# Time blocks padded to 80 rows instead of 96, first-batch inputs in arrays of their own, and routed rows kept 130 elements apart

## The chip, the cores and the metric

One NeuronCore of a Trainium2 chip runs the whole program. The metric is the device time of one execution in microseconds, taken as the median of several runs. A profile is one further execution, seen by the hardware profiler; its engines are PE (TensorE, the matrix engine), PEld (TensorE's weight loads), DVE (VectorE), ACT (ScalarE), POOL (GpSimd) and SP (SyncE, which here only issues DMAs).

## What is computed

A long convolution by FFT, a gate, and a mixture of experts with two levels of top-1 routing. Sizes: 4 batches, 10048 positions (79 blocks of 128, the last one half empty), 128 channels, 16 experts of width 1024, all in float32.

```python
h = relu(pos_emb @ w1) @ w2 * exp(-0.01 * pos)          # the filter, one for all batches
u = x * v
y = irfft(rfft(u, 2S) * rfft(h, 2S))[:S]                # along the positions
a = (x * y).reshape(B * S, D)                           # 40192 tokens
g = argmax(a @ w_group); e = argmax(a @ w_expert[g])    # with softmax weights of each
out = softmax_g * softmax_e * (relu(a @ w1[g, e]) @ w2[g, e])
```

## The kernel before

The transform is split in two steps of matmuls: one over the blocks (79 blocks, padded to `NR` rows, stand on the partitions), one over the 128 positions within a block. The program goes through these stages:

- `network` (to 43 us): the filter's small MLP for `NR` x 128 positions, in 16 groups of `4 * NR` columns. Matmuls `psh` (4 * NR columns wide) and `psg` (256 wide).
- filter transform (to 118 us): `dft_blocks` (matmuls `psa`) and `dft_positions` (`psb`), whose results DVE scales into tiles `hs`; SP stores them to `hspec` in DRAM.
- for batch b = 0 to 3, a forward stage and a middle stage. Forward: `product` loads x and v (`xv_in`) and multiplies, `fold` adds and subtracts halves into `eo`, PE does `psa`; from batch 1 on the inverse of the batch before (`inverse_blocks`, which makes `xy`, x times y) is woven in. Middle: `psb`, DVE multiplies by the filter (tiles `t`), POOL adds (`y`, lines 661 and 664), PE goes back (`pbp`, line 673) five pairs of frequencies later.
- in the middle stage of batch b + 1, `chosen` stores the rows of batch b's `xy` to DRAM (`xyd`) and computes the router; `ranked` works out each token's address. In the stages after that, `stage` loads four rows per partition of `xyd` into a tile `stg` (a unit; four buffers), POOL copies the token's number and weight beside each row (line 370) and `put` scatters the rows into pages of one expert (`prow`), by indirect DMAs of POOL.
- an inverse for the last batch (to 912 us), its routing, and from 944 us the experts, page by page.

Batch 0 differs in two ways. Its loads from channel `FIRST` (15) on go into tiles `x0` (6 channels) and `v0` (3 channels), taken out of `xv_in`, where x and v alternate in runs of 128 elements; and POOL makes two of three folds (lines 486 and 488), DVE the third.

The order of the instructions on each engine is set when the program is built: a scheduler places each instruction by what it depends on, and `keep_in_program_order`, `between` and `beyond` hold some of them to the order of the code. At run time each engine goes through its list in order. SP's list holds nearly all loads. `stage(k + 1)` is called at the first row of unit k, so a unit's copy on POOL stands ahead of the four scatters of the unit before it.

Of the kernel before, what the change touches and what calls it, by code (L numbers as in the profile page):

```python
# [12 lines left out]
F32 = mybir.dt.float32  # L13
# [11 lines left out]

SEQ, D, NB, N1 = 10048, 128, 79, 157
KM = 64
NR = 96

NN = N1 * 128  # L30
NE, G, EG, FF = 16, 4, 4, 1024
# [14 lines left out]
RW = 130  # L46
# [103 lines left out]
class Kernel:  # L150
# [60 lines left out]
    def conv(self, ctx, right):  # L211
        tc, nc, d = self.tc, self.nc, self.d
# [20 lines left out]
        xyp = ctx.enter_context(tc.tile_pool(name="xy", bufs=1, reuse_waits="tile"))  # L233
# [5 lines left out]
        for b in range(self.nbat + 1):  # L239
            last = b == self.nbat  # L240
            if last:
                ahead.close()
                inner.close()
                self.sp = ctx.enter_context(tc.tile_pool(name="stream", bufs=2, reuse_waits="tile"))
                weights = self.first_weights(right)
            if b > 0:
                xy = xyp.tile([128, NB, D], F32, tag="xy", name=f"xy{b - 1}")
            parts = groups(D, GD) if not last else []
            if b == 1:
                self.router_consts()  # L250
            self.run_ahead(b, 0, made, folded)
            for j, (d0, n) in enumerate(OUTS):
                if b > 0 and j % 2 == 0:
                    tts = self.turned(d0, min(2 * GI, D - d0))
                for i in range(2 * j, min(2 * j + 2, len(parts))):
                    self.run_ahead(b, i, made, folded)
                    self.scatter(1 + (i >= 12 and i % 2))
                    self.dft_blocks(*folded[i])
                    if b > 0 and i % 2 == 0:
                        if j % 2 == 0:  # L260
                            pos = self.inverse_rest(min(2 * GI, D - d0), tts)
                        self.inverse_blocks(b - 1, xy, d0, n, tts, pos[j % 2], j % 2)
                if last:
                    if j % 2 == 0:
                        pos = self.inverse_rest(min(2 * GI, D - d0), tts)
                    self.inverse_blocks(b - 1, xy, d0, n, tts, pos[j % 2], j % 2)
                    next(weights, None)
                    if j == 8:
                        self.scatter(sum(1 for s in self.scatters if s[0] < self.nbat - 2))
                        self.all[0].load(self.rows)  # L270
                for _ in range(3 if last else 1):
                    next(routing, None)
                if last:
                    self.scatter(1 + j % 2)
            made, folded = [], []
            if b > 0:
                oh = self.rp.tile([128, NE, NB], F32, tag="oh", name="oh")
                en = self.entries.tile([128, NB, 2], F32, tag="en", name="en")
                routing = chain(self.chosen(b - 1, xy, oh, en), self.ranked(b - 1, oh, en))
                if last:  # L280
                    for _ in range(CHOSEN):
                        next(routing)
            if not last:
                back = []
                for i, (k0, n) in enumerate(groups(NB, 2)):
                    back.append(self.middle(b, k0, n))
                    if len(back) > LAG:
                        self.back(*back.pop(0))
                    if b == 1 and i % 4 == 1:
                        self.clear_rest(i // 4)  # L290
                    self.scatter(i % 4 != 3, False)
                    if i % 4 != 3 if i < 30 else i in (31, 33):
                        next(routing, None)
                    if i >= 36:
                        self.run_ahead(b + 1, i - 36 - AHEAD - 1, made, folded)
                for args in back:
                    self.back(*args)
                for _ in range(2):
                    next(routing, None)
# [60 lines left out]
    def stage(self, k):  # L360

        while self.staged <= min(k, len(self.units) - 1):
            u = self.units[self.staged]
            n = u.n
            u.rows = self.entries.tile([128, UB, RW], F32, tag="stg", name="stg", bufs=STG)
            src = self.d["xyd"][u.b * 128 * NB : (u.b + 1) * 128 * NB].rearrange("(p t) c -> p t c", p=128)
            ins = self.nc.sync.dma_start(u.rows[:, :n, 0:128], src[:, u.t0 : u.t0 + n])
            if self.sent is not None:
                self.after(ins, self.sent)
            self.beyond(self.nc.gpsimd.tensor_copy(u.rows[:, :n, 128:130], u.en[:, u.t0 : u.t0 + n]))  # L370
            self.staged += 1
# [72 lines left out]
    def product(self, b, d0, n):  # L444

        nc, d = self.nc, self.d
        src = d["xv_in"][b, :, d0 : d0 + n]
        if b == 0 and d0 >= FIRST:

            queue = nc.gpsimd if d0 < FIRST + GI else nc.sync  # L450
            if (d0 - FIRST) % GI == 0:
                self.x0 = self.ap.tile([NR, GI, 128], F32, tag="load", name="x0", bufs=NLOAD)
                m = min(GI, D - d0)
                queue.dma_start(self.x0[:, :m], d["xv_in"][b, :, d0 : d0 + m, 0])
            tag, bufs = ("spec", NSPEC) if d0 // GD % 9 < 4 else ("tt", NTT)
            vt = self.sp.tile([NR, GD, 128], F32, tag=tag, name="v0", bufs=bufs)[:, :n]
            queue.dma_start(vt, src[:, :, 1])
            o = (d0 - FIRST) % GI
            xt = self.x0[:, o : o + n]
        else:  # L460
            xv = self.ap.tile([NR, GD, 2, 128], F32, tag="load", name="xv", bufs=NLOAD)
            nc.sync.dma_start(xv[:, :n], src)
            xt, vt = xv[:, :n, 0], xv[:, :n, 1]
            if b > 0:
                self.minus[d0] = xv[:, :n].rearrange("p d a q -> p d (a q)")
        first = b == 0 and d0 < FIRST
        self.in_turn(b, (nc.gpsimd if first else nc.vector).tensor_tensor(xt, xt, vt, ALU.mult))
        return xt, b, d0, n
# [327 lines left out]
    def chosen(self, b, xy, oh, en):  # L796


        nc, d, rp = self.nc, self.d, self.rp
# [4 lines left out]
        for u in range(len(units) + 2):  # L804
            if u < len(units):
                t0, n = units[u]
                nc.sync.dma_start(rows[:, t0 : t0 + n], xy[:, t0 : t0 + n])
                pt = self.psT.tile([128, 4, 128], F32, tag="pt", name="ptr")
                for i in range(n):
                    nc.tensor.transpose(pt[:, i], xy[:, t0 + i], self.ident)  # L810
                xts[u] = self.sp.tile([128, 4, 128], F32, tag="oo", name="xrt", bufs=2)
                nc.scalar.copy(xts[u][:, :n], pt[:, :n])
            if 0 < u <= len(units):

                n, xt = units[u - 1][1], xts.pop(u - 1)
# [12 lines left out]
            if u > 1:  # L828
                t0, n = units[u - 2]
# [27 lines left out]
    def ranked(self, b, oh, en):  # L857
# [92 lines left out]
        flat = lambda t: t.rearrange("p e t -> p (e t)")  # L950
        for h in range(4):
            es = slice(h * 4, h * 4 + 4)
            f = rp.tile([128, 4, NB], F32, tag="big1", name="f")


            first = oh[:, es, 0:1].rearrange("p e t -> p (e t)")
# [272 lines left out]
class Idle:  # L1229

    real, n, steps = False, 1, 4
# [161 lines left out]
def build(nbat):  # L1393
    import concourse.bacc as bacc

    nc = bacc.Bacc("TRN2", target_bir_lowering=False, num_devices=1, dynamic_dma_scratch_size=8192)
    shapes = {
        "xv_in": (nbat, NR, D, 2, 128),
        "x_out": (nbat, 128, D * NB),
        "pos_t": (128, 64 * NR),  # L1400
        "p_w1": (128, 128),
        "p_w2": (128, 256),
        "w_router": (128, 32),
        "m_w1": (128, NE, FF),
        "m_w2": (128, NE, FF),
        "c_iota": (128, 2 + NE + sum(PZ)),
    }
    for n, a in make_consts().items():
        shapes[n] = a.shape
    d = {n: nc.dram_tensor(n, s, F32, kind="ExternalInput").ap() for n, s in shapes.items()}  # L1410
    d["out"] = nc.dram_tensor("out", (nbat * 128 * NB, D), F32, kind="ExternalOutput").ap()
    d["prow"] = nc.dram_tensor("prow", (Pages(nbat).n * TP, RW), F32, kind="Internal").ap()
    d["xyd"] = nc.dram_tensor("xyd", (nbat * 128 * NB, D), F32, kind="Internal").ap()
    d["hspec"] = nc.dram_tensor("hspec", (128, NB, 2, 128), F32, kind="Internal").ap()
    with tile.TileContext(nc) as tc:
        Kernel(tc, d, nbat).emit()
    return nc


def layout(x, v, pos_emb, w1, w2, moe_w_group, moe_w_expert, moe_w1, moe_w2):  # L1420
# [21 lines left out]
    def twice(a):  # L1442
# [2 lines left out]

    m = {
        "xv_in": c(np.stack([xb[:, :, q], vb[:, :, q]]).transpose(1, 2, 4, 0, 3)),
        "x_out": c(
            np.concatenate(
                [xb[:, :NB, p][..., chan[d0 : d0 + n]].transpose(0, 2, 1, 3).reshape(nbat, 128, -1) for d0, n in OUTS], 2  # L1450
# [36 lines left out]
```

## Time and profile before

| | us |
|---|---|
| median of 3 runs | 1947.93 (1946.37 to 1948.35) |
| profiled execution, its own time | 1945.94 |
| span of the profiled execution | 1944.2 |
| PE busy in it | 1852.0 |
| DVE, ACT, POOL busy in it | 1458.0, 1317.4, 1086.7 |

The span runs from the first to the last instruction; the 1.7 us between it and the execution's own time lie around it. Busy times are sums over stages with different limits; matmuls overlap one another, so that a busy PE need not be a full one. The profiled execution was 2.0 us faster than the median of the runs.

### The profile page before, as it was taken

The numbers are of one execution on the slowest core, as the hardware profiler recorded it, in microseconds if no ns is written. First come the engines' busy times: TensorE is split into PE (matmuls) and PEld (weight loads), VectorE is DVE, ScalarE is ACT, GpSimd is POOL, SyncE is SP. The second block draws the span as 40 slices with busy tenths as digits, with TensorE's granted clock in tenths as the row PEclk, the third lists the DMA queues.
The fourth block names the chain that finished last, engine by engine and source line by source line (L and its number), as shares of the span: only waits on it lengthen the run. The fifth ranks groups of instructions, "written<-read, shape, count | busy, mean of one in ns | idle before, by whom it ended". The sixth has DMA issues, their size and how long they took to land.

```text
span 1944.2 us, 44476 instructions
## 1 busy us (share of the span) xinstructions
PE 1852.0 (95%) x14494; PEld 1567.9 (81%) x14494; DVE 1458.0 (75%) x3102; ACT 1317.4 (68%) x3017; POOL 1086.7 (56%) x1225
## 2 busy tenths in 40 slices
PE   8988999989999899978899999999999999999997
PEld 7966878778877687766788888888888888899997
DVE  6577767688768976893789777777777777778885
ACT  6653378447843685446777777777777777788886
POOL 3237710664799568967255556666664333355554
PEclk9999999999999999999899999999999999999999
DMA  4599976988998799857653344444343222234332
GB/s 145 199 283 252 306 188 191 350 267 263 282 326 289 233 265 343 302 186 241 218 194 112 118 128 127 164 133 131 121 131 98 90 94 97 79 119 128 122 121 77
DMA packets 234433, 365.19 MB, mean 188 GB/s; under 512 B 29687, under 2 KB 113634, under 8 KB 234192
## 3 DMA queue, kind: packets, MB, share of 16 engines
q1 hardware_dynamic: 198960, 286.90, 47.9%
q0 software_dynamic: 25728, 59.82, 8.9%
q10 hardware_dynamic: 9504, 15.54, 2.9%
q8 instruction: 117, 1.92, 0.4%
q14 instruction: 124, 1.02, 0.2%
HBM read 272.15 MB, written 91.03 MB: 187 GB/s over the span
## 4 chain that ended last, share of the span: by engine, by line
PE 66%; DVE 10%; DMA 4%; ACT 4%; issue 3%; POOL 2%; SPq 0%; ACTq 0%; DVEq 0%; POOLq 0%
PE ph L1334 8%; PE ph L1336 8%; PE py L1354 8%; PE ph L1335 8%; PE py L1356 8%; PE py L1355 8%; PE psb L497 4%; PE pbp L673 3%; PE ptm L1368 2%; PE px L1289 2%; PE po L728 2%; DMA xv<-xv_in 2%; PE po L707 2%; DMA bt<-c_b 1%; DVE t L660 1%
## 5 line engine op out<-in xcount | busy, mean ns | idle before, releaser
L1343 DVE SCALAR_TENSOR_TENSOR hl<-ph,hh 128x512 fp32r<-128x512 f32 x656 | 450.4, 687 | 172.1 <-ACT hh L1342 167.2
L1380 POOL DMA_INDIRECT out<-os,to x328 | 324.6, 990 | 384.1 <-ACT os L1375 309.6
L1342 ACT ACTIVATE hh<-ph 128x512 fp32r<-128x512 f32 x656 | 395.4, 603 | 157.5 <-PE ph L1336 134.8
L378 POOL DMA_INDIRECT prow<-stg,adr x316 | 326.3, 1032 | 122.6 <-issue 53.9
L1334 PE MATMUL ph<-xh,wh 128*128 128x512 f32 (+1 forms) x808 | 301.2, 373 | 2.2 <-ACT wh L1316 2.2
L1336 PE MATMUL ph<-xh,wl 128*128 128x512 f32 (+1 forms) x808 | 284.4, 352 | 0.0
L1354 PE MATMUL py<-hh,wh 128*128 128x512 f32 (+1 forms) x808 | 283.5, 351 | 0.0
L1335 PE MATMUL ph<-xl,wh 128*128 128x512 f32 (+1 forms) x808 | 283.4, 351 | 0.0
L1356 PE MATMUL py<-hh,wl 128*128 128x512 f32 (+1 forms) x808 | 283.0, 350 | 0.0
L1355 PE MATMUL py<-hl,wh 128*128 128x512 f32 (+1 forms) x808 | 282.2, 349 | 0.0
L661 POOL TENSOR_TENSOR y<-t 128x256 f32<-128x256 f32 (+1 forms) x160 | 121.1, 757 | 141.0 <-DVE t L660 136.4
L412 PE MATMUL psa<-fa,eo 96*64 96x158 f32 x2048 | 182.1, 305 | 12.6 <-POOL eo L486 5.7
L680 ACT COPY z<-pbp 128x512 f32<-128x512 f32 x128 | 74.8, 585 | 160.5 <-PE pbp L673 155.7
L673 PE MATMUL pbp<-y,bp 128*128 128x256 f32 x632 | 164.7, 384 | 12.7 <-POOL y L664 12.7
L497 PE MATMUL psb<-z,bt 128*128 128x256 f32 x640 | 161.8, 384 | 10.6 <-DMA bt<-c_b 3.9
L1336 PEld LDWEIGHTS ph<-xh,wl 128*128 128x128 f32 x808 | 153.6, 190 | 21.2 <-DVE wl L1323 0.2
L1355 PEld LDWEIGHTS py<-hl,wh 128*128 128x128 f32 x808 | 153.2, 190 | 20.9
L1356 PEld LDWEIGHTS py<-hh,wl 128*128 128x128 f32 x808 | 153.1, 189 | 20.7
L1354 PEld LDWEIGHTS py<-hh,wh 128*128 128x128 f32 x808 | 153.0, 189 | 20.3
L412 PEld LDWEIGHTS psa<-fa,eo 96*64 96x64 f32 x2048 | 143.2, 138 | 32.0 <-POOL eo L486 9.2
L1334 PEld LDWEIGHTS ph<-xh,wh 128*128 128x128 f32 x808 | 154.0, 191 | 17.3 <-ACT wh L1316 2.4
L1335 PEld LDWEIGHTS ph<-xl,wh 128*128 128x128 f32 x808 | 154.5, 191 | 14.9
(233 smaller groups left out, 3771.4 us busy)
## 6 DMA issues: line engine op xcount, KB each, us to landing
ws<-m_w SPq DMA_DIRECT2D x202, 256.0 KB
ht<-hspec SPq DMA_DIRECT2D x156, 256.0 KB
xv<-xv_in SPq DMA_DIRECT2D x131, 288.0 KB
bt<-c_b SPq DMA_DIRECT2D x95, 256.0 KB
bp<-c_bp SPq DMA_DIRECT2D x76, 256.0 KB
xyd<-xy SPq DMA_DIRECT2D x76, 256.0 KB
stg<-xyd SPq DMA_DIRECT2D x76, 256.0 KB
xg<-prow SPq DMA_DIRECT2D x63, 260.0 KB
```

The source lines that it names most:

```text
L378: ins = self.nc.gpsimd.indirect_dma_start(self.d["prow"], bass.IndirectOffsetOnAxis(ap=u.adr[:, t : t + 1], axis=0), u.rows[:, t - u.t0], ...
L412: ins = nc.tensor.matmul(ps[hs, i], eo[:, i, hs], self.fa[:, h], start=True, stop=True)
L497: nc.tensor.matmul(ps[:, i].rearrange("p s d -> p d s"), bt[:, i], self.frequency(k0 + i, 1)[:, :, 0], start=True, stop=True,)
L1334: k.fix(nc.tensor.matmul(ph[:, j], wh, self.xh, start=True, stop=False))
L1335: k.fix(nc.tensor.matmul(ph[:, j], wh, self.xl, start=False, stop=False))
L1336: k.fix(nc.tensor.matmul(ph[:, j], wl, self.xh, start=False, stop=True))
L1342: k.fix(nc.scalar.activation(hh, ph, AF.Relu))
L1343: k.fix(nc.vector.scalar_tensor_tensor(hl, ph, 0.0, hh.bitcast(F32), ALU.max, ALU.subtract))
L1354: k.fix(nc.tensor.matmul(self.py, wh, hh, start=(c == 0), stop=False))
L1355: k.fix(nc.tensor.matmul(self.py, wh, hl, start=False, stop=False))
L1356: k.fix(nc.tensor.matmul(self.py, wl, hh, start=False, stop=(c == NC - 1)))
L1380: ins = k.nc.gpsimd.indirect_dma_start(k.d["out"], bass.IndirectOffsetOnAxis(ap=self.to[:, h : h + 1], axis=0), o, None, bounds_check=k.nt ...
```

## The change

`NR` becomes 80. That changes the width of `psh` and of the operations around it from 384 to 320 columns, the rows of every load of x and v and of `pos_t` and `c_win`, and the rows of the transform's first step from 96 to 80. Batch 0 reads x and v from `x0_in` and `v0_in`, in which a partition's channels follow each other, so that a load moves one run of 3072 or 1536 bytes per partition instead of runs of 512. `xy`, `xyd` and the load into `stg` get rows of 130 elements; the two added columns are set to 0 by a memset on POOL, once per batch, and a load into `stg` moves one run of 2080 bytes per partition instead of four of 512. The tile `f` of `ranked` shares the memory of `lg` instead of having its own.

```diff
-NR = 96
+NR = 80
...
             if b > 0:
-                xy = xyp.tile([128, NB, D], F32, tag="xy", name=f"xy{b - 1}")
+                xy = xyp.tile([128, NB, RW], F32, tag="xy", name=f"xy{b - 1}")
+                nc.gpsimd.memset(xy[:, :, D:], 0.0)
...
             src = self.d["xyd"][u.b * 128 * NB : (u.b + 1) * 128 * NB].rearrange("(p t) c -> p t c", p=128)
-            ins = self.nc.sync.dma_start(u.rows[:, :n, 0:128], src[:, u.t0 : u.t0 + n])
+            ins = self.nc.sync.dma_start(u.rows[:, :n], src[:, u.t0 : u.t0 + n])
             if self.sent is not None:
                 self.after(ins, self.sent)
             self.beyond(self.nc.gpsimd.tensor_copy(u.rows[:, :n, 128:130], u.en[:, u.t0 : u.t0 + n]))
...
-                queue.dma_start(self.x0[:, :m], d["xv_in"][b, :, d0 : d0 + m, 0])
+                queue.dma_start(self.x0[:, :m], d["x0_in"][:, d0 : d0 + m])
...
-            queue.dma_start(vt, src[:, :, 1])
+            queue.dma_start(vt, d["v0_in"][:, d0 : d0 + n])
...
-                    nc.tensor.transpose(pt[:, i], xy[:, t0 + i], self.ident)
+                    nc.tensor.transpose(pt[:, i], xy[:, t0 + i, 0:D], self.ident)
...
-            f = rp.tile([128, 4, NB], F32, tag="big1", name="f")
+            f = rp.tile([128, 4, NB], F32, tag="lg", name="f", bufs=1)
...
+        "x0_in": (NR, D, 128),
+        "v0_in": (NR, D, 128),
...
-    d["xyd"] = nc.dram_tensor("xyd", (nbat * 128 * NB, D), F32, kind="Internal").ap()
+    d["xyd"] = nc.dram_tensor("xyd", (nbat * 128 * NB, RW), F32, kind="Internal").ap()
```

Two places of POOL's list change. The first is in the forward stage of batch 0, after the folds of the first four groups that use `x0` tiles. In brackets stand the semaphores that a row waits for: DMAHW are landings of DMAs that SP or ACT issued, DMASW those of POOL's own, the others are engines. Before:

```order
L486 TENSOR_TENSOR eo<-x_1651 96x3x64 [waits DVE_49,DMAHW5_49,PE_49,Pool_49]
L486 TENSOR_TENSOR eo<-x_1651 96x3x64 [waits DVE_49,PE_49,Pool_49]
L488 TENSOR_TENSOR eo<-x_1651 96x3x64
L486 TENSOR_TENSOR eo<-x_1683 96x3x64 [waits DVE_49,DMAHW1_49,PE_49,Pool_49]
L486 TENSOR_TENSOR eo<-x_1683 96x3x64 [waits DVE_49,PE_49,Pool_49]
L488 TENSOR_TENSOR eo<-x_1683 96x3x64
```

After:

```order
L487 TENSOR_TENSOR eo<-x_1651 80x3x64 [waits DVE_49,DMAHW5_49,PE_49,Pool_49]
L487 TENSOR_TENSOR eo<-x_1651 80x3x64 [waits DVE_49,PE_49,Pool_49]
L489 TENSOR_TENSOR eo<-x_1651 80x3x64
L248 MEMSET xy_3003 128x79x2 [waits DMAHW4_49,DMAHW3_49,DMAHW5_49,DMAHW2_49,DMAHW6_49,DMAHW1_49,DMAHW7_49,DMAHW0_49,Activation_49]
L194 DMA wr<-w_router 128x32
L196 DMA tri<-c_tri 128x128
L203 DMA idc<-c_id 128x79
L487 TENSOR_TENSOR eo<-x_1683 80x3x64 [waits DVE_49,DMAHW1_49,PE_49,Pool_49]
L487 TENSOR_TENSOR eo<-x_1683 80x3x64 [waits DVE_49,PE_49,Pool_49]
L489 TENSOR_TENSOR eo<-x_1683 80x3x64
L205 DMA iota<-c_iota 128x30
```

The first memset of `xy` now stands among the folds, with a wait for loads and stores of the filter stages, whose memory `xy` takes; the router's four loads of constants (`wr`, `tri`, `idc`, `iota`), which stood behind the last `y` of batch 0's middle stage, have moved here with it. The other three memsets stand in the middle stages of batches 1 to 3, behind the 26th pair's line 661.

The second place is any unit of scattered rows. Before:

```order
L370 COPY stg<-en 128x4x2
L378 DMA prow<-stg,adr 64768x130 [waits DMAHW4_49,DMASW1_49,Pool_49]
L378 DMA prow<-stg,adr 64768x130 [waits DMASW2_49,Activation_49]
L378 DMA prow<-stg,adr 64768x130 [waits DMASW3_49,Activation_49]
L378 DMA prow<-stg,adr 64768x130 [waits DMASW4_49]
L370 COPY stg<-en 128x4x2
L378 DMA prow<-stg,adr 64768x130 [waits DMASW5_49,DMAHW2_49,Activation_49,Pool_49]
```

After:

```order
L371 COPY stg<-en 128x4x2 [waits DMAHW2_49]
L379 DMA prow<-stg,adr 64768x130 [waits DMASW1_49,Pool_49]
L379 DMA prow<-stg,adr 64768x130 [waits DMASW2_49,Activation_49]
L379 DMA prow<-stg,adr 64768x130 [waits DMASW3_49,Activation_49]
L379 DMA prow<-stg,adr 64768x130 [waits DMASW4_49]
L371 COPY stg<-en 128x4x2 [waits DMAHW5_49]
L379 DMA prow<-stg,adr 64768x130 [waits DMASW5_49,Activation_49,Pool_49]
```

The wait for the landing of a unit's load (DMAHW) has moved from that unit's first scatter to its copy, four scatters earlier in the list, since the load now writes the columns that the copy fills too. The order of the rest of DVE's, ACT's and PE's lists is the same but for swaps of neighbours in `network`.

## Rows read from the trace of the kernel before

**Rows 1.** Windows by stage: busy us (instructions), granted clock, DMA share, GB/s.

```profile
0.00:43.00 43.00, 36.07 (x240) 32.14 (x240) 28.05 (x67) 30.87 (x83) 16.49 (x21) 1.00 0.51 158
...
78.00:118.00 40.00, 37.11 (x160) 30.27 (x161) 32.07 (x99) 35.52 (x125) 12.65 (x18) 0.96 0.93 318
118.00:172.00 54.00, 45.79 (x496) 36.17 (x497) 43.83 (x85) 21.70 (x72) 39.45 (x57) 0.97 1.11 248
...
944.00:1944.00 1000.00, 985.22 (x5508) 854.55 (x5508) 754.73 (x1526) 771.74 (x1592) 530.89 (x544) 0.99 0.39 123
```

**Rows 2.** Waits, 118 to 172 us: total, times, longest.

```profile
DVE x L467 <- DMA v<-xv_in: 9.9, 13, 2.1
...
PE psa L412 <- POOL eo L486: 5.7, 10, 1.9
```

**Rows 3.** Timeline of PE in `network`: start, duration, count.

```profile
19.54 0.69 PE L523 MATMUL psh<-p,w 128*128 128x384 f32 x3
20.06 1.57 PE L523 MATMUL psg<-w,h 128*96 128x256 f32 x12
```

**Rows 4.** Waits of DVE, 78 to 122 us.

```profile
DVE hs L635 <- DMA hspec<-hs: 5.4, 7, 2.8
```

**Rows 5.** Timeline of DVE, first and last products of batch 0.

```profile
121.64 1.00 DVE L467 TENSOR_TENSOR x<-x,v 96x384 f32<-96x384 f32 x2
122.57 0.34 DVE L488 TENSOR_TENSOR eo<-x 96x192 f32<-96x192 f32 x1
...
169.66 1.21 DVE L467 TENSOR_TENSOR x<-x,v 96x384 f32<-96x384 f32 x2 [0.54 <-DMA v<-xv_in]
```

**Rows 6.** Groups of DVE, 118 to 172 us: count, busy, mean ns, idle before.

```profile
L467 DVE TENSOR_TENSOR x<-x,v 96x384 f32<-96x384 f32 (+1 forms) x38 | 25.2, 684 | 10.2 <-DMA v<-xv_in 9.9
```

**Rows 7.** Timeline of POOL in the same stage, two pieces.

```profile
127.97 1.35 POOL L486 TENSOR_TENSOR eo<-x 96x192 f32<-96x192 f32 x2 [0.65 <-DVE x L467]
...
130.15 1.56 POOL L486 TENSOR_TENSOR eo<-x 96x192 f32<-96x192 f32 x2
...
150.19 1.56 POOL L486 TENSOR_TENSOR eo<-x 96x192 f32<-96x192 f32 x2
...
152.63 1.57 POOL L486 TENSOR_TENSOR eo<-x 96x192 f32<-96x192 f32 x2
154.17 0.58 POOL L488 TENSOR_TENSOR eo<-x 96x192 f32<-96x192 f32 x1
```

**Rows 8.** Timeline of POOL: the first and last of four router loads.

```profile
246.79 0.60 POOL L194 DMA_DIRECT2D wr<-w_router  x1
...
248.46 0.54 POOL L205 DMA_DIRECT2D iota<-c_iota  x1
```

**Rows 9.** Timeline of SP: first load into filter memory, a unit's load, a filter load.

```profile
126.30 0.35 SPq L230 DMA_DIRECT2D fi<-c_fi  x1
...
517.31 0.39 SPq L367 DMA_DIRECT2D stg<-xyd  x1
...
540.79 1.28 SPq L649 DMA_DIRECT2D ht<-hspec  x1
```

**Rows 10.** Timeline: that unit's copy on POOL; the filter load's user on DVE.

```profile
519.35 0.21 POOL L370 COPY stg<-en 128x8 f32<-128x8 f32 x1
...
546.95 0.69 DVE L660 TENSOR_TENSOR t<-psb,ht 128x512 f32<-128x512 f32 x1 [4.09 <-DMA ht<-hspec]
```

**Rows 11.** First `y` and first `pbp` of batch 2's middle, then batch 3's.

```profile
540.03 0.75 POOL L664 TENSOR_TENSOR y<-t 128x256 f32<-128x256 f32 x1
...
542.92 1.02 PE L673 MATMUL pbp<-y,bp 128*128 128x256 f32 x4
...
746.13 0.76 POOL L664 TENSOR_TENSOR y<-t 128x256 f32<-128x256 f32 x1
...
749.48 1.02 PE L673 MATMUL pbp<-y,bp 128*128 128x256 f32 x4
```

**Rows 12.** Window after PE waits of 2.2 and 1.1 us: PE busy, clock.

```profile
437.90:441.30 3.40, 2.93 (x14) 0.50 0.71 225
```

More of the change, by code (lines that the diff above doesn't have):

```diff
@@ L1447, in layout @@
         "xv_in": c(np.stack([xb[:, :, q], vb[:, :, q]]).transpose(1, 2, 4, 0, 3)),
+        "x0_in": c(xb[0][:, q].transpose(0, 2, 1)),
+        "v0_in": c(vb[0][:, q].transpose(0, 2, 1)),
         "x_out": c(
```

## The prediction

> **What bounds the kernel now.** I read the windows by stage first. In the experts, 944 to 1944 us, PE is busy 985 of 1000 us [rows 1]: that half is PE's, no line of the change touches it, and it gets no term. In `network` PE is busy 36.07 of 43 us, more than ACT's 30.87 or DVE's 28.05, so a narrower `psh` counts there in full. In the two stages in which batch 0's inputs are read the DMA share is 0.93 and 1.11 and PE is busy 37.11 of 40 and 45.79 of 54 us: there the loads matter.
>
> Next the chain of waits from 118 to 172 us. DVE's products (line 467) wait 9.9 us for loads of v; PE waits 5.7 us for POOL's folds [rows 2], and POOL's folds wait for products or follow each other without a gap. So the chain is load, product, fold, `psa`, and what DVE waits for a load reaches PE, as far as POOL, which stands between, has time to spare. That is the first place on which the sum rests. The second is where forward turns into middle in batches 2 and 3. POOL scatters rows up to there and then has to make the first `y`, for which PE's first `pbp` waits.
>
> **Network.** Three `psh` of 384 columns take 20.06 − 19.54 = 0.52 us [rows 3]. At 320 columns a sixth goes, 0.087 us; 16 groups make −1.4 us. `psg` (12 in 1.57 us) moves 256 columns for each block as before and only its weights shrink, which saves nothing. The narrower operations of ACT, DVE and POOL ahead of the first group and behind the last give an estimated 0.3 us. Term −1.7; bounds 0 (ACT or DVE is the limit) and −2.3 (every operation ahead of PE's first shrinks by a sixth).
>
> **Loads during the filter.** Eight loads of 288 KB run between 78 and 118 us. A sixth less is 8 × 48 KB = 0.39 MB, at the stage's 318 GB/s [rows 1] 1.2 us of DMA time. DVE waits 5.4 us there for stores of `hs` [rows 4], which share the DMA engines with these loads, so I take most: −0.9, bounds 0 and −1.2.
>
> [...] No row here compares the two sizes.
>
> **Batch 0's forward stage.** 38 products stand in pairs, 19 of them, and each pair's group of folds gives POOL two additions and a subtraction, DVE the other subtraction. The first pair starts at 121.64, the last at 169.66 [rows 5]: 48.02/18 = 2.67 us each. What would a pair take with no wait for a load? Where POOL goes back to back, it needs 2.18 us (127.97 to 130.15) and 2.44 us (150.19 to 152.63) [rows 7], on average 2.31; I take 2.35, nearer the later one, for there the products run beside it as they will. Of 2.67 that saves 0.32, over 18.5 pairs −5.9 us. It can't be more than DVE's whole wait, −9.9, and it is 0 if the products slow down as they close up (below). That the waits shrink I take from the packets: a load of `v0` becomes one run of 1536 bytes per partition, a third of the descriptors, and 80 rows; the share of 1.11 at 248 GB/s is far below the 318 GB/s of the stage before, so the engines are held by pieces, not bytes.
>
> Into POOL's list come the memset and four router loads. The loads took 246.79 to 249.00 = 2.2 us in their old place [rows 8]; a memset of 128x79x2 is not in the trace; between the copy of 128x8, 0.21 [rows 10], and a fold of 0.58 [rows 7] I take 0.3. POOL is the limit once loads are early: +2.5. It is 0 if it falls in idle time of POOL, at least 0.65 us of which stands before single folds [rows 7]. The memset also waits for filter memory to be free. SP's `fi` load into that memory went out at 126.30 [rows 9], and POOL reaches the place behind the second group, 127.3 or so; a wait of up to 1 us is inside the bounds. Behind it stand all later folds. Net −3.4, bounds +2.5 and −9.9.
>
> **The units' copies.** The copy now waits for its own load; behind it on POOL stand four scatters, then everything up to the first `y` of the middle. In batch 2, at the worst unit that I found, SP issued the load at 517.31 and POOL copied at 519.35 [rows 9, 10], 2.0 us later. A load's latency: `ht` was issued at 540.79 and DVE started on it at 546.95 [rows 9, 10], 6.2 us at most (DVE waited 4.09 of them). So the copy waits up to 4.2 us, at least 0 if a load of one run lands in 2 us; I take 3, nearer the first, as that row is a measured landing. Such a delay is not made up before the middle, as scatters follow each other without waiting. At the middle, batch 2's first two `y` ended at 540.78 and PE's first `pbp` started at 542.92, 2.1 us to spare; in batch 3 746.89 and 749.48, 2.6 us [rows 11]. Lost: 3 − 2.1 and 3 − 2.6, together +1.3. [...]
>
> **At nothing.** The memsets of batches 1 to 3 (an estimated 0.3 us each) stand behind the 26th pair of a middle stage, in which POOL is not what PE waits for past its start; without that cover they cost 0.9. `f` on `lg`'s memory comes later in DVE's own order than `lg`'s last use. The first step's contraction over 80 rows instead of 96 leaves `psa`'s columns as they were. The stores of `xyd` get 520 bytes per row instead of 512 and the loads of `stg` fewer pieces, both off the path but at the copies.
>
> **Sum.** −1.7 − 0.9 − 3.4 + 1.3 = −4.7 us: the profiled execution's 1945.94 becomes 1941.2, and the median, which lay 2.0 us above it, 1943.2. About 0.2%, 3.9 us, is what the measurement can tell from no change.
>
> **Rivals.**
>
> *A: the sum above*, 1943.2, likeliest at 0.42. Its own range is 1940 to 1946, so of it 0.24 is faster and 0.18 the same.
>
> *B: batch 0 gains nothing.* The products took 684 ns on average [rows 6], but the first two, at 121.64, 500 each [rows 5]; folds back to back took 0.78 in pairs and 0.58 alone [rows 7]. DVE and POOL slow each other, and with loads out of the way each would merely be slower. Then −1.7 − 0.9 + 2.5 + 1.3 = +1.2: 1949.1. Against it: if they excluded each other wholly, a pair would need 1.00 + 0.34 of DVE and 3 × 0.58 of POOL, 3.08 us, and it took 2.67 with waits. Chance 0.25, same.
>
> [...]
>
> *C: POOL's copies wait for whole latencies* (slower). If SP's loads go out as POOL reaches the copy, each first copy waits S = 6.2 us, not 3. Then (6.2 − 2.1) + (6.2 − 2.6) + 2 × 1.7 = 11.1 against gains of 6.0: +5.1, 1953.0. It decides from S = 5.6 on, where 2S − 1.3 = 6.0 + 3.9. For it: PE waited 1.1 and 2.2 us for `y` elsewhere and lost its clock. Against it: the load was 2 us ahead. Chance 0.11.
>
> *D: the waits for v vanish entirely* and POOL's new work falls in its idle time: −1.7 − 0.9 − 9.9 + 1.3 = −11.2, 1936.7. That is 2.67 − 9.9/18.5 = 2.13 us per pair, just under the shortest stretch of POOL seen (2.18). Chance 0.22, faster.
>
> That the change doesn't do what it says is rival B's first half: loads as late as before.
>
> **Numbers.** Faster 0.24 + 0.22 = 0.46, the same 0.18 + 0.25 = 0.43, slower 0.11. Range 1936.0 to 1950.5: it holds A and B and most of D, and leaves C and D's far end out.
>
> **What would show it.** In the windows 0 to 43 becomes about 41.3, three `psh` 0.43 us. From 118 to 172 us DVE's wait for `v0` is under 4 us and pairs stand 2.35 us apart; if the wait is gone and pairs still stand 2.6 apart with products near 800 ns, B is right. Waits of POOL's copy for `xyd` show near 507 to 537 and 715 to 745, of 3 us; waits of `pbp` for `y` at the start of batches 2 and 3, with a clock of 0.5 behind them, show C. What would make it wrong most easily: a memset that waits long for filter memory with all folds behind it, or stretches of half clock that appear or vanish for another reason.

## The result and the profile after

The changed kernel is slower: 1959.14 us median of 6 runs (1956.45 to 1967.07) against 1947.83 of the kernel before, ratio 1.0071 (95% interval 1.0048 to 1.0095): 0.7% and clear of noise. The profiled execution has a span of 1954.7 us, 10.5 more than before. The forecast was 1943.2 us, in a range to 1950.5.

Windows of the changed kernel, cut at its own stages: the filter's `psa`, then the forward stage of batch 0 in two pieces, then the experts. The columns are those of [rows 1].

```profile
40.80:75.90 35.10, 34.57 (x512) 34.28 (x512) 15.21 (x43) 13.57 (x44) 0.00 (x0) 1.00 0.34 114
113.80:122.00 8.20, 6.25 (x74) 5.01 (x74) 6.27 (x17) 3.97 (x15) 4.04 (x7) 1.00 0.98 336
122.00:184.00 62.00, 61.34 (x444) 53.99 (x445) 44.20 (x72) 18.27 (x60) 41.57 (x60) 0.51 0.63 166
956.00:1954.70 998.70, 983.83 (x5504) 853.22 (x5504) 753.28 (x1520) 770.14 (x1591) 528.83 (x544) 0.99 0.38 123
```

The third line is the result. For 62 us PE is busy 61.34, the DMA share has fallen from 1.11 [rows 1] to 0.63, and the granted clock is 0.51: PE works at about half its full clock to the stage's end. What bounds the stage now is PE at half clock. The first line has the same instruction, `psa` over 80 rows, at clock 1.00 for 35 us on end, so 80 rows alone did not make the clock fall there. The timeline of PE in the changed kernel shows what it did before and after:

```profile
113.85 4.74 PE L413 MATMUL psa<-fa,eo 80*64 80x158 f32 x60 [0.17 <-DVE hs L639]
118.93 0.48 PE L413 MATMUL psa<-fa,eo 80*64 80x158 f32 x2 [0.34 <-POOL eo L487]
120.86 1.03 PE L413 MATMUL psa<-fa,eo 80*64 80x158 f32 x12 [1.45 <-DVE eo L489]
122.19 58.64 PE L413 MATMUL psa<-fa,eo 80*64 80x158 f32 x438 [0.30 <-POOL eo L489]
181.29 4.05 PE L498 MATMUL psb<-z,bt 128*128 128x256 f32 x11 [0.46 <-ACT z L426]
```

At full clock PE waits 1.45 us, and short times more; the clock falls about 123 us; then come 438 matmuls without one wait (the trace holds two records for each matmul of the code), and it does not rise. It is 1.00 again from some 3 us after the first `psb` (128 rows, 128 columns of weights). In the kernel before, PE waited more in this stage, and the clock fell too, for 3.4 us from 140.9 on; it came back under `psa` over 96 rows. Its windows there, and PE's timeline:

```profile
136.00:140.90 4.90, 3.43 (x40) 2.73 (x40) 2.97 (x6) 1.34 (x5) 3.21 (x5) 1.00 1.22 232
140.90:144.30 3.40, 3.40 (x30) 3.37 (x28) 2.26 (x6) 1.15 (x4) 2.63 (x5) 0.50 1.23 230
144.30:150.00 5.70, 5.14 (x57) 3.74 (x53) 4.43 (x10) 2.04 (x8) 3.91 (x6) 1.00 1.24 233
```

```profile
140.38 7.56 PE L412 MATMUL psa<-fa,eo 96*64 96x158 f32 x72 [1.47 <-POOL eo L486]
```

Which wait lets the clock fall is not shown: in the same profile a wait of 1.92 us ahead of 124.62 left it at 1.00.

The waits of the same stretch, 118 to 172 us, answer to [rows 2]:

```profile
ACT z L426 <- PE psa L413: 38.4, 27, 3.2
...
DVE z L426 <- PE psa L413: 9.1, 5, 2.7
...
DVE x L468 <- DMA v<-v_in: 1.9, 1, 1.9
PE psa L413 <- DVE eo L489: 1.5, 1, 1.5
```

DVE's wait for loads of v went from 9.9 to 1.9 us, and DVE and ACT now wait for PE. A stage that PE holds up gives the loads more time, so this alone does not show that they are quicker; the kernel with 96 rows below, whose clock comes back, has 2.7 us.

The other loss is on POOL, ahead of the middle stages of batches 2 and 3. Timeline of POOL in the changed kernel, the three copies of batch 2's forward stage that waited, and the first `y`:

```profile
486.75 0.19 POOL L371 COPY stg<-en 128x8 f32<-128x8 f32 x1 [1.36 <-DMA stg<-xyd]
...
494.72 0.33 POOL L371 COPY stg<-en 128x8 f32<-128x8 f32 x1 [2.39 <-DMA stg<-xyd]
...
507.33 0.19 POOL L371 COPY stg<-en 128x8 f32<-128x8 f32 x1 [1.21 <-DMA stg<-xyd]
...
550.51 0.74 POOL L662 TENSOR_TENSOR y<-t 128x256 f32<-128x256 f32 x1
```

And PE there, `pbp` and the first `psb` of the stage:

```profile
543.74 2.88 PE L498 MATMUL psb<-z,bt 128*128 128x256 f32 x12
...
551.99 1.13 PE L674 MATMUL pbp<-y,bp 128*128 128x256 f32 x4 [1.19 <-POOL y L665]
```

The first `y` comes 6.8 us after the first `psb`, and PE waits for it. In the kernel before it came 3.3 us after (the `y` just ahead of the row in [rows 11]), and `pbp` did not wait:

```profile
536.04 2.87 PE L497 MATMUL psb<-z,bt 128*128 128x256 f32 x12
...
539.35 0.76 POOL L661 TENSOR_TENSOR y<-t 128x256 f32<-128x256 f32 x1
```

Seven of the runs below came on chips on which every kernel, the one before too, ran some 9 to 11% longer, all of it from batch 2's forward stage on (before: 2131 to 2159 us); of these only ratios within a chip and stages ahead of that point are used.

### The profile page after: what moved, and what is told of

Same layout as the page of the kernel before. It is cut to its first block, busy times and chain, and to the rows that moved or that the text cites. A ratio compares the mean times of both kernels' runs of the same rounds, so it can differ in the third digit from the quotient of the medians.

```text
span 1954.7 us, 44464 instructions
## 1 busy us (share of the span) xinstructions
PE 1871.5 (96%) x14494; PEld 1588.6 (81%) x14494; DVE 1460.4 (75%) x3102; ACT 1314.1 (67%) x3017; POOL 1085.8 (56%) x1229
## 3 DMA queue, kind: packets, MB, share of 16 engines
q8 instruction: 117, 1.92, 0.4%
## 4 chain that ended last, share of the span: by engine, by line
PE 57%; DVE 3%; ACT 2%; issue 2%; POOL 2%; DMA 1%; SPq 0%; ACTq 0%; POOLq 0%; DVEq 0%
PE ph L1335 8%; PE py L1355 8%; PE py L1357 8%; PE ph L1337 8%; PE py L1356 8%; PE ph L1336 8%; PE ptm L1369 2%; PE px L1290 2%; PE pbp L674 1%; PE po L729 1%; PE psb L498 1%; PE po L708 1%; PE ptr L811 1%; PE pt L696 1%; POOL prow L379 1%
## 5 line engine op out<-in xcount | busy, mean ns | idle before, releaser
L413 PE MATMUL psa<-fa,eo 80*64 80x158 f32 x2048 | 199.7, 338 | 6.5 <-DVE eo L481 3.4
L674 PE MATMUL pbp<-y,bp 128*128 128x256 f32 x632 | 167.0, 388 | 18.0 <-POOL y L665 18.0
L413 PEld LDWEIGHTS psa<-fa,eo 80*64 80x64 f32 x2048 | 162.8, 157 | 24.0 <-issue 7.0
```

What stands on the lines that cost most here:

```text
L413: ins = nc.tensor.matmul(ps[hs, i], eo[:, i, hs], self.fa[:, h], start=True, stop=True)
L674: nc.tensor.matmul(by_part[:, i], bp[:, i], y[:, i], start=True, stop=True,)
```

## The experiments

**Theory "rows"**: in batch 0's forward stage `psa` over 80 rows doesn't bring PE's clock back once it has fallen, and over 96 rows it does. **Rival "start"**: the loads and waits at the stage's start decide, whatever the rows. Beside them **"copies"**: POOL's early wait for a unit's load costs the middles of batches 2 and 3.

### Batch 0 with 96 rows again

```diff
+N0 = 96
-self.x0 = self.ap.tile([NR, GI, 128], ...)      # v0, eo of these groups, x0_in, v0_in, fa alike
+self.x0 = self.ap.tile([N0, GI, 128], ...)
```

> The changed kernel, but x0, v0, their folds and psa of batch 0's groups from channel 15 on have 96 rows again (rows 80 to 95 are zeros); the order of every engine's list is that of the changed kernel. The changed kernel ran from 123 to 184 us at a granted clock of 0.50 while PE had no wait. Theory 'rows': psa over 80 rows does not bring PE's clock back and over 96 rows it does. Then batch 0's forward stage has at most some 8 us at 0.50, psb of batch 0 starts near 166 instead of 181.3, and the time is 1943 (1938 to 1947). Theory 'start': the clock falls for the wait of 1.45 us at 119 us and for how the loads come, whatever the rows; then it stays at 0.50 and the time is 1958 to 1960.

1948.86 us (1943.58 to 1951.15), ratio 1.0006 (0.9993 to 1.0019). Windows of this kernel:

```profile
120.00:128.00 8.00, 6.05 (x50) 5.46 (x51) 6.85 (x11) 1.85 (x6) 6.14 (x11) 0.57 0.76 234
128.00:169.00 41.00, 35.42 (x400) 27.92 (x397) 40.43 (x62) 16.03 (x52) 37.84 (x51) 1.00 0.98 262
```

Timeline of its PE at the same place:

```profile
119.59 0.48 PE L414 MATMUL psa<-fa,eo 96*64 96x158 f32 x2 [0.71 <-POOL eo L488]
122.02 8.22 PE L414 MATMUL psa<-fa,eo 96*64 96x158 f32 x70 [1.95 <-DVE eo L490]
```

The clock falls at the same place, about a longer wait (1.95), and is back by 128 us. The rows added hold zeros, so it was not what they hold that brought it back: the fall lasted 6.8 us with 96 rows and 61.4 with 80. The forward stage, first `psa` to first `psb`, takes 56.1 us instead of 67.4. "Start" is out: it had 1958 to 1960 and a clock that stays low. "Rows" is right on the clock and too low on the time: it had 1938 to 1947 and `psb` near 166 us, which came at 170.2.

It is not one profile alone. The mean clock of the whole execution was 0.982 to 0.988 in this kernel's ten runs and 0.966 to 0.972 in the changed kernel's six. Of the 17 profiles in this document with 96 rows in this stage, 16 show a fall in it, and each was over after 3.4 or 6.8 us; in the changed kernel it lasted 61.4 us. What happens between 80 and 96 rows was not tried.

### Rows of 80 alone, and own arrays alone

```diff
-NR = 96
+NR = 80
```

> The kernel before with NR = 80 alone: loads in runs of 512 bytes, xy in rows of 128. Theory 'rows': the waits for v and for folds, 9.9 and 5.7 us, are still there, one of them drops the clock as at 139 us before, and it then stays at 0.50 to psb: forward stage 60 to 67 us, time 1952 to 1962. Theory 'start': no long stretch at 0.50; network and filter give 4 us, so 1942 to 1945.

1955.13 us (1946.63 to 1960.07), ratio 1.0029 (1.0011 to 1.0047). Two of its ten runs took 1946.6 and 1946.7 with a mean clock over the span of 0.982, the other eight 1952.1 to 1960.1 with 0.967 to 0.973. In the profiled one:

```profile
113.90:122.00 8.10, 6.16 (x76) 5.48 (x78) 6.80 (x20) 4.17 (x15) 3.63 (x4) 0.96 0.90 308
122.00:180.30 58.30, 57.88 (x439) 57.34 (x435) 38.47 (x67) 17.97 (x60) 37.55 (x54) 0.50 0.80 173
```

The fall lasted 64.9 us here. So the smaller row count does it without the arrays, and it hangs on whether the clock falls, which by its mean it did not do for long in the two runs near 1946.6.

```diff
-queue.dma_start(self.x0[:, :m], d["xv_in"][b, :, d0 : d0 + m, 0])
+queue.dma_start(self.x0[:, :m], d["x0_in"][:, d0 : d0 + m])       # and v0, 96 rows
```

> The kernel before with x0_in and v0_in alone, 96 rows. Theory 'rows': a fall of the clock is made good within some 8 us; DVE's wait for v0 falls from 9.9 to under 3 us and the forward stage gets 4 to 9 us shorter: 1938 to 1944. Theory 'start': a stretch at 0.50 to the end of the stage, 1954 to 1960. If the products slow down as they close up (rival B of the prediction): 1946 to 1949.

1942.07 us (1939.63 to 1948.85), ratio 0.9974 (0.9958 to 0.9990): faster. DVE's wait for `v0` from 117 to 170 us:

```profile
DVE x L467 <- DMA v<-v_in: 5.0, 6, 1.8
```

It falls to 5.0, not under 3, and the forward stage takes 53.5 us instead of 56.0.

### PE given wide matmuls

```diff
+if b == 0 and 14 <= d0 // GD < 16:
+    for _ in range(12):
+        nc.tensor.matmul(ps[:, 0, 0:128], self.ident, self.ident, start=True, stop=True)
```

> The changed kernel with 24 matmuls of 128 rows, 128 columns of weights and 128 moving columns added among psa of the 15th and 16th group of batch 0's forward stage, near 138 us; their results are overwritten, so only PE's work grows. Theory 'rows' (the clock stays low since 80 rows are too little work for PE, not for a wait): the granted clock is back at 1.00 within some 6 us of them, psb of batch 0 starts 8 to 12 us earlier than 181.3, and the time is 1948 to 1953. If the clock falls again behind them, or the cause is another, it stays near 0.50 and the 24 matmuls add 3 to 6 us: 1961 to 1965.

1954.71 us (1951.39 to 1958.57), ratio 1.0039 (1.0024 to 1.0055), 4.4 us below the changed kernel by the medians (6.2 by the ratios, each on its own chip) though PE has more to do. Timeline of PE and two windows:

```profile
121.53 11.76 PE L416 MATMUL psa<-fa,eo 80*64 80x158 f32 x82 [0.30 <-POOL eo L492]
133.22 1.22 PE L412 MATMUL psa<-ident 128*128 128x128 f32 x4
...
144.23 9.60 PE L416 MATMUL psa<-fa,eo 80*64 80x158 f32 x134
```

```profile
122.00:135.00 13.00, 13.00 (x86) 10.86 (x82) 13.00 (x19) 3.70 (x12) 11.46 (x19) 0.50 0.98 234
...
140.00:175.00 35.00, 32.17 (x376) 27.60 (x375) 29.40 (x50) 13.43 (x44) 26.82 (x37) 1.00 0.59 179
```

The 24 wide matmuls are 48 records in the trace. 82 records over 80 rows took 11.76 us, 143 ns each; behind the wide ones 134 took 9.60, 72 ns each. The clock is back at 138.8 us, 5.6 us after the first wide one, and stays at 1.00 to the end over the same 80 rows and through short waits. `psb` starts at 174.3 instead of 181.3, 7 us and not the 8 to 12 expected, and the time lies just above the 1948 to 1953 of "rows". The mean clock of the nine runs was 0.977 to 0.985.

### Rows of 130, whole and mended

```diff
-xy = xyp.tile([128, NB, D], F32, ...)
+xy = xyp.tile([128, NB, RW], F32, ...)        # memset, xyd, load of stg, f on lg as in the change
```

> The kernel before with rows of 130 in xy, xyd and stg alone, so with the copies' waits, the memsets and the router's loads among the folds. By the changed kernel's trace the copies wait 5.0 and 4.1 us and PE waits 8.8 and 6.3 us for y in the middles of batches 2 and 3 (3.5 and 4.7 before). Theory 'copies': that costs 3 to 6 us, and the router's loads up to 2.5 in batch 0: 1951 to 1956. Theory 'nothing': the units' smaller piece count or PE's own slack hides it: 1946 to 1950.

1956.01 us, ratio 1.0038 (1.0023 to 1.0052), and once more on another chip:

> Rows of 130 alone once more, as the base of the other two on the same chip: slower than the kernel before by 5 to 9 us where that runs near 1947.

1953.96 us, ratio 1.0043 (1.0026 to 1.0060). This part alone costs 7.4 to 8.1 us by the medians. In its middle of batch 2 PE waits longest for the first `y`:

```profile
550.89 1.13 PE L674 MATMUL pbp<-y,bp 128*128 128x256 f32 x4 [2.47 <-POOL y L665]
```

Then the mends, alone and together:

```diff
 # late copy: in put, not in stage
+if t == u.t0:
+    self.beyond(self.nc.gpsimd.tensor_copy(u.rows[:, : u.n, 128:130], u.en[...]))
 # in order
-nc.gpsimd.memset(xy[:, :, D:], 0.0)
+self.tc.keep_in_program_order(nc.gpsimd.memset(xy[:, :, D:], 0.0))
```

> Rows of 130 alone (which by themselves gave 1956.0, ratio 1.0038), but each unit's copy stands right ahead of that unit's own first scatter, four scatters later, so that POOL waits for a load where the kernel before waited for it. Theory 'copies': the middles of batches 2 and 3 were 2.5 and 3.6 us longer because POOL came late to the first y; that goes, 1949 to 1951. Theory 'memset and router': the loss is that of batch 0 (forward 2.5 us and middle 3.1 us longer), and this stays at 1954 to 1957.

1954.43 us, ratio 1.0040 (1.0027 to 1.0052).

> Rows of 130 alone, but the memsets are kept to the order of the code, so that the first one and the router's four loads stand behind the last y of batch 0's middle again and no longer among its folds; the copies still wait. Theory 'copies': 1953 to 1957, for the copies hold POOL as before. Theory 'memset and router': 1949 to 1952.

1954.14 us, ratio 1.0039 (1.0025 to 1.0053).

> Rows of 130 with both mends. Theory 'two causes': within 3 us of the kernel before. Theory 'a third cause': 4 us or more above it, near the run with rows of 130 alone.

1950.46 us, ratio 1.0030 (1.0017 to 1.0043), on the chip on which rows of 130 alone had 1.0043.

Neither mend alone shows in the time: each run came out where the theory had it that blames the other part. In the trace the late copy does its work: no copy waits, the first `y` stands 3.3 us after the first `psb` again (8.0 with rows of 130 alone):

```profile
546.10 0.75 POOL L663 TENSOR_TENSOR y<-t 128x256 f32<-128x256 f32 x1
```

The middle of batch 3, first `psb` to the next stage's first `po` (a matmul of the inverse), took 108.0 to 109.8 us (mean 108.8) in the profiles of the six kernels with early copies and 105.0 to 108.4 (mean 106.2) in the seven others, slower chips left out. That is 2.6 us, and 0.9 in batch 2 (to the next stage's first `psa`), where the means are 110.5 and 109.6 and the ranges overlap. But the kernel with late copies alone has the 108.4 itself, among the six: that the copies are a cause is shown by the late first `y` and PE's wait for it, their price of some 3.5 us is not. They are not the whole: with both mends 3.9 us over the kernel before are left by the medians, 5.8 by the ratio (3.3 to 8.4).

A third piece shows in POOL's list. With the wider `xy` POOL's first load of v waits for PE's `psb`: with rows of 130 alone it goes out at 117.28 us in one profile, where the kernel before has 92.30. All profiles with the wide `xy`, that of the tile alone (below) too, have 113.1 to 117.4, the others 88.4 to 92.3. That the memory of the `v0` tiles has moved with it is inferred. In the changed kernel:

```profile
113.97 0.53 POOL L458 DMA_DIRECT2D v<-v_in  x1 [24.96 <-PE psb L498]
...
115.61 0.52 POOL L458 DMA_DIRECT2D v<-v_in  x1
```

The filter's `psb` and batch 0's forward stage together took 95.7 to 99.0 us (mean 96.8) in the nine kernels with a wide `xy` and 96 rows, and 95.7 and 95.8 in two profiles of the kernel before: 1 us, with ranges that touch. Four more runs were to settle the rest, all on the slower chips:

> Rows of 130 alone with both mends: copies ahead of their own unit's first scatter, memsets in the order of the code. Each by itself took only 0.6 and 2.0 us off the mean of 1955.0. Theory 'two causes that overlap': with both gone the loss of 7.5 us goes, 1947 to 1950. Theory 'a third cause' (rows of 520 bytes in memory, or the lists of SP and DVE as they come out): it stays at 1951 to 1954.

> Rows of 130 alone with both mends once more, since the chip of the call before ran every kernel, the one before too, some 9% longer from the third batch on, and its ratio (0.9941) is not to be compared with the others. Theory 'two causes that overlap': 1947 to 1950. Theory 'a third cause': 1951 to 1954.

Ratios 0.9941 (0.9918 to 0.9963) and 0.9970 (0.9943 to 0.9997): on those chips the mended rows of 130 gain. Why the sign differs from that of 1.0030 above is not known.

> The kernel before with only the tile xy (and f on lg's memory, without which it doesn't fit) as in the change: rows of 130 in xy, but xyd and the loads into stg in rows of 128, no memset, the copies as before. POOL's first load of v0 waits for stores of hs as in all kernels with the wide xy. Theory 'moved memory': 3 to 6 us above the kernel before, of which some 2 in batch 0's forward stage. Theory 'the loads or xyd': within 2 us of it.

```diff
-nc.sync.dma_start(rows[:, t0 : t0 + n], xy[:, t0 : t0 + n])
+nc.sync.dma_start(rows[:, t0 : t0 + n], xy[:, t0 : t0 + n, 0:D])
```

Ratio 1.0003 (0.9974 to 1.0032).

> Rows of 130 in xy and xyd with the memsets in the order of the code, but the loads into stg take only the 128 columns, in four runs of 512 bytes per partition, so that the copies need not wait for them and stand where they stood. Theory 'moved memory': 3 to 6 us above the kernel before, as with both mends. Theory 'the loads in one run': within 2 us of it.

```diff
-ins = self.nc.sync.dma_start(u.rows[:, :n], src[:, u.t0 : u.t0 + n])
+ins = self.nc.sync.dma_start(u.rows[:, :n, 0:128], src[:, u.t0 : u.t0 + n, 0:128])
```

Ratio 1.0037 (1.0006 to 1.0068). Neither is narrow enough to tell the theories apart, and the scatters that the loads feed run in just the stages that were longer. The remainder stays open.

> The kernel before itself, for a second profile: each theory expects its stages within 1 us of the first one, batch 0's middle stage (75.9 us there, 75.2 to 79.4 in the other kernels) perhaps more.

Ahead of batch 2 its stages agree within 0.7 us with the first profile, but for batch 0's middle, 79.0 instead of 75.9 us: in that stage a difference of 3 us between two profiles means nothing.

### The parts put together

> The whole change with three things mended: 96 rows in batch 0 (which gave 1948.9), the copies ahead of their own unit's first scatter, the memsets in the order of the code. If copies and memsets cost the 6 to 7 us that rows of 130 cost by themselves, 1940 to 1943, below the kernel before by 5 to 8 us. If what is left of the change gains nothing, 1946 to 1949.

1944.04 us (1935.98 to 1947.44), ratio 0.9985 (0.9970 to 1.0000): between the two forecasts, and a gain that can hardly be told from none.

Without rows of 130, with rows of 80 and own arrays of 96 rows:

> Rows of 80 and batch 0's own arrays with 96 rows there, without rows of 130. From the runs so far: own arrays alone gave 1943.5 in the mean, four below before; the changed kernel with 96 rows in batch 0 gave 1948.3, and rows of 130 alone cost 7.5. If the parts add, 1940 to 1942. If rows of 80 save nothing outside batch 0, 1943 to 1945.

Ratio 0.9993 (0.9971 to 1.0016), and 0.9998 (0.9971 to 1.0025) in a repeat, on slower chips:

> Rows of 80 and own arrays with 96 rows in batch 0, without rows of 130, once more for the same reason. If the parts add, 1940 to 1942; if rows of 80 save nothing outside batch 0, 1943 to 1945.

> Rows of 80 and own arrays with 96 rows in batch 0, without rows of 130. If the parts add, 6 to 8 us below the kernel before; if rows of 80 save nothing outside batch 0, 3 to 5 us.

1936.38 us (1932.25 to 1941.40), ratio 0.9954 (0.9934 to 0.9974). It beats the kernel before by 10.2 us on its chip by the medians (9.0 by the ratio): 5.8 from the arrays, on another chip, so some 4.4 from rows of 80 elsewhere. On the slower chips the gain is not seen in the time, but the part ahead of batch 0's middle is as short there: the first `psb` of batch 0 starts at 166.6 to 167.0 us in all three profiles, where two of the kernel before have 174.0 and 173.8.

## Why the prediction was wrong, step by step

The step that failed stands under **At nothing**: "The first step's contraction over 80 rows instead of 96 leaves `psa`'s columns as they were." The columns are as they were, and at full clock so is the time (35.1 us from the filter's first `psa` to its first `psb` in both kernels). But once the clock had fallen in batch 0's forward stage, the number of rows decided whether it came back within it: the fall lasted 61.4 us with 80 rows, to 3 us behind the first `psb`, and 6.8 with 96. Price: 1959.14 against 1948.86, 10 us by the medians and 12.7 by the ratios; the first `psb` of batch 0 came 11.1 us later (181.3 against 170.2). The prediction named a stretch of half clock "for another reason" as what could make it wrong, but priced none in this stage, though the kernel before showed a fall there (140.9 us) that was over after 3.4 us.

**Network**, −1.7: 43.0 to 40.8 us, −2.2; right. Three `psh` in the changed kernel take 19.86 − 19.43 = 0.43 us, as forecast:

```profile
19.43 0.60 PE L524 MATMUL psh<-p,w 128*128 128x320 f32 x3
19.86 1.56 PE L524 MATMUL psg<-w,h 128*80 128x256 f32 x12
```

**Loads during the filter**, −0.9: the stage's mean over the profiles is 39.1 us with 96 rows (38.3 to 40.0 in twelve) and 38.2 with 80 (37.4 to 38.7 in eight), −0.9. DVE's wait for stores of `hs` fell from 5.4 [rows 4] to 1.6 (3.3 to 2.0 in the mean over the same profiles). The means bear the term out, though the ranges overlap and no run changes these loads alone.

**Batch 0's forward stage**, −3.4, of which −5.9 was the pairs' (2.35 us apart) and +2.5 POOL's added work: mechanism right, the pairs' part mis-sized. The kernels with 96 rows and own arrays lack the added work, and in them the stage takes 52.6 to 53.5 us instead of 56.0: 2.5 to 3.4 gained and not 5.9. Pairs stand 2.45 us apart where they run evenly (154.87 to 162.21 are three) and 2.47 to 2.50 from the first to the last, since the products slow down as they close up (from 684 to 817 ns in the mean). Rows of the kernel with rows of 80 and own arrays of 96, to be read against [rows 6]:

```profile
L468 DVE TENSOR_TENSOR x<-x,v 96x384 f32<-96x384 f32 (+1 forms) x38 | 29.9, 817 | 3.3 <-DMA v<-v_in 3.3
```

684 ns became 817 as the wait went from 9.9 to 3.3: of 6.6 us less waiting, 4.7 went into longer products. That is rival B's direction, not its size. With the added work, in the changed kernel with 96 rows, the stage took 56.1 us, so that the net term came out at nothing:

```profile
L469 DVE TENSOR_TENSOR x<-x,v 96x384 f32<-96x384 f32 (+1 forms) x38 | 32.3, 879 | 2.7 <-DMA v<-v_in 2.7
```

There pairs stand 2.63 us apart with products over 800 ns, the sign that the prediction named for rival B; but the added work and 6.8 us at half clock lie in it too, and what each of the three takes is not separated. POOL's added work took 2.4 us, as good as priced (124.17 to 125.99 and 0.55 at 127.96 in the changed kernel), and its wait for filter memory did not show.

**The units' copies**, +1.3: mechanism right, term mis-sized. It took S = 3 us once for each batch; the copies waited 5.0 us in three and 4.1 us in two, and the first `y` came 3.5 and 3.8 us later behind the first `psb` than before. Less the slack of 2.1 and 2.6 us that leaves 2.6, and PE's waits at the first `pbp` were 1.19 and 1.09, together 2.3. By the means of the stages it would be 3.5 us, which no run's time shows. Rival C's sum adds 1.7 us of half clock for each stall. No run shows that term: behind these two waits the granted clock was 1.00 (550 to 564 and 755 to 770 us), and so it was behind the 2.47 us with rows of 130 alone.

**Not seen at all**: the first `v0` load that goes out some 25 us later, a third place of POOL's list that changed beside the two that were named, 1 us. What else rows of 130 cost is open.

The sign came from `psa` over 80 rows. With 96 rows there the change stood 1 us above the kernel before (1948.86, ratio 1.0006: no change that can be told), inside the range and near rival B's 1949.1, but in part for other reasons: 10.2 us of gain, 7.4 to 8.1 of loss in rows of 130, and some 3 that the sum of the parts, taken across chips, leaves unexplained. That it fell so near B's number is luck.

## What to carry to other kernels

A matmul over fewer rows is not free because its columns stay: ask what happens to it at half clock, and whether the stage has anything that brings the clock back (here it stayed at half for 61.4 us with 80 rows and for 6.8 with 96). Where a tile grows, compare the waits of all loads in the lists, not only those of the instructions that the diff names, since other tiles can wait for something else from then on (here a load that went out 25 us later). A wait that is moved ahead of work on a queue that runs without gaps is paid at each occurrence, up to the next slack (here copies that waited 1.36, 2.39 and 1.21 us in one stage, with 2.1 us of slack behind them).

## What the runs showed of the hardware

A busy PE is not a PE at full clock. With `psa` over 80 rows and 64 columns of weights PE was busy 61.34 of 62 us at a granted clock of 0.51; over 96 rows, the added ones zeros, the clock was back after 6.8 us; with 24 matmuls over 128 rows and 128 columns it came back too, 5.6 us after the first of them, and it then stayed at 1.00 over 80 rows.
